# Thirty-eight matmuls instead of 39 per unit of the gate and up products: features split 192, 64, 192

## The chip, the cores and the metric

The kernel runs as one program on one core of one Trainium2 chip. Times are device microseconds (us) of one execution; the kernel before took 699.87 us (median of 3 runs, 699.38 to 700.0). The profile is of one further execution. Engines are named as the profile names them: PE (matrix multiplies), PEld (the loads of its stationary operand), DVE (vector), ACT (scalar, activation), POOL (general), SP (issues the DMAs).

## The reference

One block of a transformer, on x of 2048 tokens by 448 features, all in fp32. First a Fourier mixing layer, real part only, and a residual; then a gated feed-forward layer (GEGLU, 448 to 1792 to 448 features) and a residual:

```python
n = layernorm(x)
a, b = n @ dft_hid_re.T, n @ dft_hid_im.T
h = x + dft_seq_re @ a - dft_seq_im @ b
m = layernorm(h)
g, u = m @ w_gate, m @ w_up
out = h + (gelu_tanh(g) * u) @ w_down
```

Matrix products on PE are made in fp16. An fp32 operand is split into a high and a low half (hi = fp16(a), lo = fp16(a - hi)), and a product of two fp32 operands is three fp16 products: hi·hi, hi·lo, lo·hi. Where a layer's sizes allow, a Strassen-like scheme makes seven block products instead of eight.

## The kernel before, in words

**Stages.** The program has four stretches in order of time. (1) The sequence transform, 64 steps (`N_STEPS`), the last 32 of them with seven products ("fast"); PE multiplies blocks of the sequence matrices (`ws`, halves made from `wr`) by the halves of the normalised x. Between its steps stand, for 7 of the 8 token pairs p, the hidden transform (`hid_mm`, 21 matmuls for each half g of the pair), the second layer norm, and the preparation of the feed-forward operands. (2) Gate and up products for token block 0 (512 tokens), 14 units t = 0 to 13, one for each slice of 128 features. (3) Gate and up for blocks 1 and 2 (256 tokens each), 28 units, with the down products between them. (4) The rest of the down products. A unit is thus 512 columns wide 14 times and 256 columns wide 28 times.

**A unit** (class `GateUp`) makes seven products into three banks X, Y and Z, in the order x1 (A11·B11), z1 (S1·T1), y1 (S2·T2), x2 (A12·B21), z2 (S4·B22), y2 (S3·T3), y3 (A22·T4), y3 after x1 and z1 of the next unit. Between two of them ACT or DVE takes the bank's value: after x1 ACT copies X to Y (L1089), and y1 adds to that copy.

**The 448 features** are the contracted dimension, split 256 and 192. Products over 256 take two slots of 128 rows and 3 terms, so 6 matmuls; products over 192 take one and a half slots and so 5 matmuls, the halves of two terms sharing one slot. Four products of 6 and three of 5 make 39.

**Operands.** Activations: for each token pair ACT writes the normalised pair to `xn` (`ffn_norm_act`), DVE makes differences in `tt` (`ffn_sums`), ACT writes high halves to `xs` (`ffn_hi`, helper `hi_part`, L108), DVE low halves (`ffn_lo`, helper `lo_part`, L112 without a scale, L114 with one), and SP transposes `xs` into `hops` (25 slots). Weights: class `Weights` loads a feature slice (`gu_raw`), makes sums on DVE (`gu_s`, L328 to L331), high halves on ACT and low halves on DVE (`gu_w`, 28 slots), and stores them. Eight slices are prepared in stretch 1, six in stretch 2.

**What sets the order.** Nothing is scheduled by a tool: the order in the code is the order of each engine's queue, and an engine runs its queue strictly in that order. In stretch 1 tables `early` and `after` attach work to a step n: `early[n]` runs after the step's own `ws` halves, `after[n, half]` after each half of the step's matmuls. The tables of slices (`DFT_F`: slice f has its sums at step n, raw halves at n+1, halves of sums at n+2) and of pairs (`ffn_sums` and `ffn_split` at n1 and n2) fill them. For the first pair n1, n2 are 22 and 23, and slice 5 has n = 22. `hid_out(p, g)` (L719 to L721 on ACT) takes the result of `hid_mm(p, g)`, and `hid_seed(p, 1)` (L711 on ACT) then puts h back into the same bank; `hid_mm(p, 1)` can begin only after that.

Of the kernel before, what the change touches and what calls it, by code (L numbers as in the profile page):

```python
# [13 lines left out]
P = 128  # L14
# [18 lines left out]
def kernel(  # L33
# [127 lines left out]
    OPS_K1 = {"B11": 0, "T1": 4, "T2": 8, "T3": 12}  # L161
    OPS_K2 = {"B21": 16, "B22": 19, "T4": 22}
    N_OPS = 25


    W_OPS = {"A11": 0, "A12": 2, "A22": 4, "S1": 6, "S2": 8, "S3": 10, "S4": 12}
# [79 lines left out]
    def ffn_sums(q, j, parts=range(4)):  # L246

        if 0 in parts:
            t = fops.tile([P, 960], F32, tag="tt", name=f"tt_{q}_{j}")
            ffn[q, j] = ffn[q, j], t  # L250
        xn, t = ffn[q, j][:2]
        sub = V.tensor_sub
        if 0 in parts:
            sub(t[:, 0:256], xn[:, 1, 0:256], xn[:, 0, 0:256])
        if 1 in parts:
            sub(t[:, 256:448], xn[:, 1, 256:448], t[:, 0:192])
            V.tensor_scalar(t[:, 448:512], t[:, 192:256], -1.0, None, op0=ALU.mult)
        if 2 in parts:
            sub(t[:, 512:704], xn[:, 1, 256:448], xn[:, 1, 0:192])
            V.tensor_scalar(t[:, 704:768], xn[:, 1, 192:256], -1.0, None, op0=ALU.mult)  # L260
        if 3 in parts:

            sub(t[:, 768:960], xn[:, 0, 256:448], t[:, 256:448])

    def ffn_views(q, j):
        xn, t, xs = ffn[q, j]
        k1 = xs[:, 0:2048].rearrange("p (o h d) -> p o h d", o=4, h=2)
        k2 = xs[:, 2048:3200].rearrange("p (o d) -> p o d", o=3)
        return xn, t, k1, k2, t[:, 0:768].rearrange("p (o d) -> p o d", o=3)

    def ffn_hi(q, j, parts=range(2)):
        if 0 in parts:
            ffn[q, j] += (fops.tile([P, N_OPS * P], F16, tag="xs", name=f"xs_{q}_{j}"),)
        xn, t, k1, k2, t3 = ffn_views(q, j)
        if 0 in parts:
            hi_part(k1[:, 0, 0, :], xn[:, 0, 0:256])
            hi_part(k2[:, 0:2, 0:192], xn[:, :, 256:448])
        if 1 in parts:
            hi_part(k1[:, 1:4, 0, :], t3)
            hi_part(k2[:, 2, 0:192], t[:, 768:960])  # L280

    def ffn_lo(q, j, parts=range(5)):
        xn, t, k1, k2, t3 = ffn_views(q, j)
        raw, t4 = (k2[:, 0:2], xn[:, :, 256:448]), (k2[:, 2], t[:, 768:960])
        if 0 in parts:
            lo_part(k1[:, 0, 1, :], xn[:, 0, 0:256], k1[:, 0, 0, :])
        if 1 in parts:
            lo_part(k1[:, 1:4, 1, :], t3, k1[:, 1:4, 0, :])
        for n, (dst, src) in ((2, raw), (4, t4)):
            if n in parts:  # L290
# [1295 lines left out]
```

## Time and profile before

| | |
|---|---|
| median of 3 runs | 699.87 us |
| span of the profiled execution, first to last instruction | 698.1 us |
| outside that span (median less span) | 1.8 us |
| PE busy | 693.5 us, 5308 matmuls |
| DVE busy | 571.2 us, 1137 instructions |
| ACT busy | 394.1 us, 781 instructions |
| POOL busy | 166.6 us |
| stretch 1, to about | 337 us |
| stretch 2, to about | 462 us |

The profiled execution has no time of its own beside the span; the 1.8 us is the difference to the median of the timed runs. In the timeline of an engine a row is: start in us, length in us, engine, line, operation, out<-in by the names of the program, shapes, and how many instructions were merged into the row; in brackets stands how long the engine was idle ahead of it and what ended that. Rows of one engine can overlap by some tens of nanoseconds, since an instruction begins before the one ahead has quite ended.

### The profile page before, as it was taken

How to read it: one execution, taken by the hardware profiler on the slowest of the kernel's cores; microseconds unless marked ns; L12 is line 12 of the kernel's file. 1: busy time of each engine (PE TensorE's matmuls, PEld its weight loads, DVE VectorE, ACT ScalarE, POOL GpSimd, SP SyncE). 2: the span in 40 equal slices, each digit the busy share in tenths (PEclk: the TensorE clock that was granted, in tenths of full speed). 3: DMA queues.
4: the chain of work that ended last, by engine and by line, in shares of the span. 5: the costliest groups of instructions: out<-in, count | busy, mean ns of one | idle time of the engine just before them, and what ended most of it. 6: DMA issues, size and time to landing. Idle time of an engine off the chain costs nothing.

```text
span 698.1 us, 13955 instructions
## 1 busy us (share of the span) xinstructions
PE 693.5 (99%) x5308; PEld 514.3 (74%) x5308; DVE 571.2 (82%) x1137; ACT 394.1 (56%) x781; POOL 166.6 (24%) x183
## 2 busy tenths in 40 slices
PE   9999999999999999999999999999999999999998
PEld 6555555555979888997644444469999999999997
DVE  6998996958999898995648797777778877899786
ACT  5876755746766555665427666555555453655631
POOL 0004754461202000000303333521120111232224
PEclk9999999999999999999999999999999999999999
DMA  8798679997968559384656877797869985887612
GB/s 272 243 244 271 143 260 268 249 251 286 194 197 189 163 125 237 127 196 178 158 187 239 286 235 247 202 325 237 234 206 334 243 300 176 313 283 273 226 50 80
DMA packets 113731, 155.81 MB, mean 223 GB/s; under 512 B 61696, under 2 KB 78208, under 8 KB 113664
## 3 DMA queue, kind: packets, MB, share of 16 engines
q1 hardware_dynamic: 113664, 154.92, 74.1%
q8 instruction: 41, 0.67, 0.4%
q14 instruction: 26, 0.21, 0.1%
HBM read 106.66 MB, written 34.34 MB: 202 GB/s over the span
## 4 chain that ended last, share of the span: by engine, by line
PE 96%; ACT 1%; DVE 1%; issue 1%; POOL 0%; ACTq 0%; POOLq 0%
PE acc L644 21%; PE acc_f L521 16%; PE acc_d L1248 15%; PE pY L1044 15%; PE pZ L1044 10%; PE pX L1044 10%; PE y L730 9%; PE pw L102 1%; ACT ws L108 1%; DVE ws L114 0%; ACT xn_h L243 0%; DVE sums L471 0%; ACT dn_w L108 0%; ACT v L974 0%; ACT y L721 0%
## 5 line engine op out<-in xcount | busy, mean ns | idle before, releaser
L1044 PEld LDWEIGHTS <-gw 128*128 128x128 f16 x1365 | 133.3, 98 | 42.7
L644 PE MATMUL acc<-xs,ws 128*128 128x448 f16 x768 | 146.9, 353 | 0.0
L521 PEld LDWEIGHTS <-ws 128*128 128x128 f16 x1344 | 128.7, 98 | 2.2 <-DVE ws L114 0.5
L644 PEld LDWEIGHTS <-ws 128*128 128x128 f16 x768 | 75.3, 98 | 70.3 <-issue 0.6
L1138 POOL TENSOR_TENSOR hs<-hs,c 128x256 f32<-128x256 f32 (+1 forms) x42 | 59.2, 1410 | 248.2 <-ACT c L1136 181.7
L1248 PE MATMUL acc_d<-wd,dn_w 128*128 128x224 f16 x1008 | 110.7, 259 | 0.0
L1248 PEld LDWEIGHTS <-dn_w 128*128 128x128 f16 x1008 | 96.9, 98 | 2.0
L521 PE MATMUL acc_f<-t,ws 128*128 128x224 f16 x768 | 92.2, 259 | 0.1
L1044 PE MATMUL pY<-hops,gw 128*128 128x256 f16 (+1 forms) x595 | 90.2, 294 | 0.0
L114 DVE SCALAR_TENSOR_TENSOR ws<-wr,ws 128x768 f16<-128x768 f32 (+2 forms) x66 | 73.8, 1119 | 10.4 <-ACT ws L108 10.1
L521 PE MATMUL acc_f<-xs,ws 128*128 128x224 f16 x576 | 73.5, 259 | 0.0
L108 ACT ACTIVATE ws<-wr 128x768 f16<-128x768 f32 (+2 forms) x66 | 60.4, 916 | 11.9 <-DMA wr<-in_w_seq_dram 11.0
L730 PE MATMUL y<-wh,z 128*128 128x448 f16 x336 | 66.2, 352 | 0.0
L1044 PE MATMUL pZ<-hops,gw 128*128 128x256 f16 (+1 forms) x385 | 61.7, 294 | 0.0
L1044 PE MATMUL pX<-hops,gw 128*128 128x256 f16 (+1 forms) x385 | 61.7, 294 | 0.0
L1089 ACT ACTIVATE pY<-pX 128x256 f32<-128x256 f32 (+1 forms) x42 | 18.4, 439 | 66.9 <-PE pX L1044 66.5
L730 PEld LDWEIGHTS <-z 128*128 128x128 f16 x336 | 32.9, 98 | 29.5 <-issue 0.3
L108 ACT ACTIVATE ws<-sums 128x512 f16<-128x512 f32 x64 | 39.0, 624 | 25.4 <-DVE sums L471 18.1
L1044 PEld LDWEIGHTS <-gu_w 128*128 128x128 f16 x273 | 26.6, 98 | 31.9
L1054 DVE SCALAR_TENSOR_TENSOR c<-pZ,u 128x256 f32<-128x256 f32 (+1 forms) x42 | 21.5, 511 | 34.7 <-PE pZ L1044 17.9
L1100 ACT ACTIVATE u<-pY 128x256 f32<-128x256 f32 (+1 forms) x42 | 19.1, 454 | 53.6 <-PE pY L1044 53.5
L112 DVE TENSOR_TENSOR dn_w<-dn_s,dn_w 128x640 f16<-128x640 f32 x48 | 42.2, 879 | 1.5 <-ACT dn_w L108 1.4
(148 smaller groups left out, 1005.1 us busy)
## 6 DMA issues: line engine op xcount, KB each, us to landing
gw<-w_dram SPq DMA_DIRECT2D x35, 896.0 KB, 6.6
wr<-in_w_seq_dram SPq DMA_DIRECT2D x100, 256.0 KB, 4.2
hid_dram<-hs SPq DMA_DIRECT2D x27, 512.0 KB, 5.9
hid<-hid_dram SPq DMA_DIRECT2D x54, 256.0 KB, 5.6
w_dram<-gu_w SPq DMA_DIRECT2D x14, 896.0 KB, 5.2
gu_raw<-in_w_gu_dram SPq DMA_DIRECT2D x28, 384.0 KB, 5.4
wr<-in_w_seq_dram SPq DMA_DIRECT2D x14, 512.0 KB, 5.7
x<-in_x_dram SPq DMA_DIRECT2D x16, 224.0 KB, 4.3
```

Source lines behind the costliest of these rows:

```text
L108: A.activation(dst, src, AF.Copy, scale=scale)
L112: V.tensor_sub(dst, src, hi)
L114: V.scalar_tensor_tensor(dst, src, scale, hi, op0=ALU.mult, op1=ALU.subtract)
L521: PE.matmul(fast_sum(n, k), fast_a(n, i, lw, a), fast_b(j, lx, b), start=j == 0 and m == 0 and k in (0, 1, 3, 5), stop=j == NT // 2 - 1 an ...
L644: PE.matmul(acc[key][:, :D], w[:, lw, block * P : (block + 1) * P], xs[c][:, lx, :], start=c == 0 and m == 0, stop=c == NT - 1 and m == 2,)
L730: PE.matmul(y[:, :D], z[p][:, lz, k, g * P : (g + 1) * P], wh[:, lw, k, :], start=p == NP - 1 and k == 0 and m == 0, stop=k == 6 and m == ...
L1044: PE.matmul(ps, w[:, wl, wa + ws, :], ops[:, m + ms, :], start=first and n == 0, stop=last and n == len(terms) - 1, skip_group_check=True,)
L1054: V.scalar_tensor_tensor(dst, ps, SC, other, op0=ALU.mult, op1=ALU.add)
L1089: A.activation(self.Y, self.X, AF.Copy)
L1100: A.activation(self.u2, self.Y, AF.Copy, scale=SC)
L1138: G.tensor_mul(c22, c22, self.cols(self.c12))
L1248: PE.matmul(ps, w[:, la, a, :], wd[n][:, lb, b, :], start=n == 0 and m == 0 and opens, stop=n == NC - 1 and m == 2, skip_group_check=True,)
```

## The change

The 448 features are split 192, 64 and 192. Every product contracts over 192, and the middle 64 rows are a further product that isn't made by itself: its three half-size terms ride in the empty halves of the slots of S1, S2 and S3's operands and of the A and S4 products. S1, S2, S3 and A11 take 5 matmuls, A12, A22 and S4 take 6 (`W_TERMS`): 38 in all. `hops` and `xs` have 27 slots.

To fill the slots the preparation changes:

- `Weights.tails` (ACT, two casts of 64 partitions) at step n-1 of a slice; one more such cast at the head of `hi(True)`; `rest` (DVE, one operation of 64 partitions) after the raw low halves. The difference L330 is 384 wide instead of 256. The halves of sums take two casts of 768 and 640 instead of two of 512 on ACT, and four operations (384, 384 on 64 partitions, 128 on 64 partitions, 256) instead of two of 512 on DVE.
- `ffn_sums` makes four differences of 192 and, as part 3, one of 64 that reads a high half already made. `ffn_split` no longer makes all high halves and then all low ones: high part 0, low part 0, high part 1, sums part 3, low parts 1 and 2, high part 2, low part 3.
- `ffn_transpose` moves 8, 3, 4 and 12 slots instead of 8, 8, 6 and 3; the plan of side work in stretches 2 and 3 is put in the new order of parts, at the same places.

The places in the order on which the prediction rests come from here. **ACT, step 23**, the high halves of the first pair (xs from xn and tt) up to the seed of the second half of pair 1 (L711, y_1). Before:

```order
L108 ACTIVATE xs_0_1459<-tt_0_1404 128x3x256
L108 ACTIVATE xs_0_1459<-tt_0_1404 128x192
L108 ACTIVATE zs_1201<-acc_10_1251 128x448
L108 ACTIVATE zs_1201<-acc_11_1252 128x448
L108 ACTIVATE ws_1509<-wr_1389 128x1024
L108 ACTIVATE gu_w_1454<-gu_s_1399 128x512 x2
L719 ACTIVATE hx_1_1268,mv_h_1_1564<-y_0_1411 128x448
L720 ACTIVATE mv_h_1_1564<-mv_h_1_1564 128x1
L721 ACTIVATE y_0_1411,mv_h_1_1564<-y_0_1411,mv_h_1_1564 128x448
L711 ACTIVATE y_1_1568<-hx_1_1268 128x448
```

Now, from the first cast of the new high part 2 (gu_raw_1395 is the next slice's raw tile):

```order
L108 ACTIVATE xs_0_1485<-tt_0_1430 128x256
L108 ACTIVATE xs_0_1485<-xs_0_1485 128x64
L108 ACTIVATE zs_1217<-acc_10_1269 128x448
L108 ACTIVATE gu_raw_1395<-gu_raw_1395 64x128 x2
L108 ACTIVATE zs_1217<-acc_11_1270 128x448
L108 ACTIVATE ws_1542<-wr_1413 128x1024
L108 ACTIVATE gu_w_1478<-gu_s_1425 128x768
L108 ACTIVATE gu_w_1478<-gu_s_1425 128x640
L754 ACTIVATE hx_1_1288,mv_h_1_1599<-y_0_1435 128x448
L755 ACTIVATE mv_h_1_1599<-mv_h_1_1599 128x1
L756 ACTIVATE y_0_1435,mv_h_1_1599<-y_0_1435,mv_h_1_1599 128x448
L746 ACTIVATE y_1_1603<-hx_1_1288 128x448
```

The first of these rows reads the last 64 columns of tt, which DVE now writes inside the split, and the second reads a low half that DVE writes; behind them stand the same zs, ws, gu_w and L719 to L721 work as before (now L754 to L756 and L746), with two casts of a raw tile between.

**DVE, the same step.** Before, from the ws low half (its differences tt stood ahead of this row):

```order
L114 SCALAR_TENSOR_TENSOR ws_1451<-wr_1334,ws_1451 128x1024
L114 SCALAR_TENSOR_TENSOR gu_w_1454<-gu_raw_1205,gu_w_1454 128x512
L114 SCALAR_TENSOR_TENSOR gu_w_1454<-gu_raw_1205,gu_w_1454 128x256
L112 TENSOR_TENSOR xs_0_1459<-xn_h_0_1355,xs_0_1459 128x256
L112 TENSOR_TENSOR xs_0_1459<-tt_0_1404,xs_0_1459 128x3x256
L112 TENSOR_TENSOR xs_0_1459<-xn_h_0_1355,xs_0_1459 128x2x64
L112 TENSOR_TENSOR xs_0_1459<-xn_h_0_1355,xs_0_1459 128x2x128
```

Now:

```order
L114 SCALAR_TENSOR_TENSOR ws_1475<-wr_1354,ws_1475 128x1024
L114 SCALAR_TENSOR_TENSOR gu_w_1478<-gu_raw_1223,gu_w_1478 128x512
L114 SCALAR_TENSOR_TENSOR gu_w_1478<-gu_raw_1223,gu_w_1478 128x256
L377 SCALAR_TENSOR_TENSOR gu_s_1425<-gu_w_1478,gu_raw_1223 64x128
L112 TENSOR_TENSOR xs_0_1485<-xn_h_0_1377,xs_0_1485 128x2x64
L112 TENSOR_TENSOR xs_0_1485<-xn_h_0_1377,xs_0_1485 128x2x192
L272 TENSOR_TENSOR tt_0_1430<-xn_h_0_1377,xs_0_1485 128x64
L112 TENSOR_TENSOR xs_0_1485<-tt_0_1430,xs_0_1485 128x3x192
```

The row L272 (sums part 3) is what ACT's cast of 256 above waits for; six DVE rows of this step now stand ahead of it.

**ACT, step 17**, slice 9's raw high halves up to the seed of the second half of pair 0. Before:

```order
L108 ACTIVATE gu_w_1184<-gu_raw_1002 128x512
L108 ACTIVATE gu_w_1184<-gu_raw_1002 128x256
L108 ACTIVATE zs_1201<-acc_00_1027 128x448
L719 ACTIVATE hx_0_980,mv_h_0_1229<-y_0_1096 128x448
L720 ACTIVATE mv_h_0_1229<-mv_h_0_1229 128x1
L721 ACTIVATE y_0_1096,mv_h_0_1229<-y_0_1096,mv_h_0_1229 128x448
L711 ACTIVATE y_1_1233<-hx_0_980 128x448
```

Now:

```order
L108 ACTIVATE gu_raw_1008<-gu_raw_1008 64x128
L108 ACTIVATE gu_w_1198<-gu_raw_1008 128x512
L108 ACTIVATE gu_w_1198<-gu_raw_1008 128x256
L108 ACTIVATE zs_1217<-acc_00_1033 128x448
L108 ACTIVATE gu_raw_1123<-gu_raw_1123 64x128 x2
L754 ACTIVATE hx_0_984,mv_h_0_1247<-y_0_1106 128x448
```

The new first row overwrites a part of the raw tile that the first of slice 9's sums on DVE (now L354) reads, so ACT waits there for DVE, which it did not before.

The diff, cut to its core:

```diff
+    W_TERMS = {
+        "A11": ((0, 0), (17, 0), (1, 1), (18, 1), (0, 2)),
+        "A12": ((3, 0), (20, 0), (2, 1), (19, 1), (3, 2), (2, 3)),
...
+        "S1": ((7, 0), (23, 0), (8, 1), (7, 2), (6, 3)),
...
     def ffn_sums(q, j, parts=range(4)):
...
-            sub(t[:, 0:256], xn[:, 1, 0:256], xn[:, 0, 0:256])
+            sub(t[:, 0:192], xn[:, 1, H1], xn[:, 0, H1])
         if 1 in parts:
-            sub(t[:, 256:448], xn[:, 1, 256:448], t[:, 0:192])
-            V.tensor_scalar(t[:, 448:512], t[:, 192:256], -1.0, None, op0=ALU.mult)
+            sub(t[:, 192:384], xn[:, 1, H1], xn[:, 1, H2])
+            sub(t[:, 384:576], xn[:, 1, H2], t[:, 0:192])
         if 2 in parts:
-            sub(t[:, 512:704], xn[:, 1, 256:448], xn[:, 1, 0:192])
-            V.tensor_scalar(t[:, 704:768], xn[:, 1, 192:256], -1.0, None, op0=ALU.mult)
+            sub(t[:, 576:768], xn[:, 0, H2], t[:, 384:576])
         if 3 in parts:
-            sub(t[:, 768:960], xn[:, 0, 256:448], t[:, 256:448])
+            xs = ffn[q, j][2]
+            sub(t[:, 768:832], xn[:, 0, RR], xs[:, 7 * P + 192 : 7 * P + 256])
...
+        if 2 in parts:
+            hi_part(t4[:, 0], t[:, 576:832])
+            hi_part(ts[:, 0, 1, 192:256], b2[:, 1, 1, 192:256])
...
     def ffn_split(q, j):
-        ffn_hi(q, j)
-        ffn_lo(q, j)
+        ffn_hi(q, j, (0,))
+        ffn_lo(q, j, (0,))
+        ffn_hi(q, j, (1,))
+        ffn_sums(q, j, (3,))
+        ffn_lo(q, j, (1, 2))
+        ffn_hi(q, j, (2,))
+        ffn_lo(q, j, (3,))
...
+        def tails(self):
+            gate, up = self.raw
+            hi_part(gate[64:, 3], gate[64:, 0])
+            hi_part(gate[64:, 0], up[64:, 3])
...
-            V.tensor_sub(s[:, 6:8], gate[:, 0:2], up[:, 0:2])
-            V.tensor_sub(s[:, 8:10], gate[:, 4:6], s[:, 4:6])
+            V.tensor_sub(s[:, 6:9], up[:, 0:3], gate[:, 0:3])
+            V.tensor_sub(s[:, 9:11], gate[:, 3:5], s[:, 3:5])
...
         def hi(self, of_raw):
             if of_raw:
                 self.w = w_tile(f"gu_w{self.f}", self.place)
+                hi_part(self.up[64:, 3], self.up[64:, 0])
...
+        def rest(self):
+            a2 = self.slots(4, 5)[64:, 0]
+            V.scalar_tensor_tensor(self.s[64:, 9], a2, -1.0 / W_SC, self.gate[64:, 3], op0=ALU.mult, op1=ALU.add)
...
+            w, s = self.slots(0, 28), self.s
+            lo_part(w[:, 23:26], s[:, 1:9:3], w[:, 7:15:3], W_SC)
+            for k in slice(8, 15, 3), slice(12, 13):
+                lo_part(w[64:, k], s[64:, k.start - 6 : k.stop - 6 : k.step], w[64:, k], W_SC)
+            lo_part(w[:, 26:28], s[:, 9:11], w[:, 15:17], W_SC)
...
         def split(self, of_raw):
             self.hi(of_raw)
             self.lo(of_raw)
+            if of_raw:
+                self.rest()
...
+        at(after, (n - 1, 0), lambda f=f: gu[f].tails())
...
-            at(early, n1, lambda b=b, j=j: ffn_sums(b, j))
+            at(early, n1, lambda b=b, j=j: ffn_sums(b, j, range(3)))
...
-        for n, (wl, ws, ms) in enumerate(terms):
+        for n, (wo, m) in enumerate(W_TERMS[a]):
             PE.matmul(
                 ps,
-                w[:, wl, wa + ws, :],
-                ops[:, m + ms, :],
+                w[:, wo, :],
+                ops[:, OPS[b] + m, :],
```

More of the change, by code (lines that the diff above doesn't have):

```diff
@@ L275, in ffn_hi @@
         if 0 in parts:
[L276 to L277 removed]
+            hi_part(b2[:, :, 0, 192:256], xn[:, :, RR])
+            hi_part(b2[:, :, 0, 0:192], xn[:, :, H2])
+            hi_part(xs[:, 0:192], xn[:, 0, H1])
         if 1 in parts:
[L279 to L284, printed above, removed]
+            hi_part(ts[:, :, 0, 0:192], t3)
@@ L1352 @@
         if w:
+            w.rest()
             w.hi(False)
```

108 lines of the change are left out of this document (54 added, 54 removed), and 4 rows, old and new, of the table W_TERMS.

## The prediction

> **What bounds the kernel now.** I read the page's first part, then PE's waits, then the chain of work that ended last, then stretches, then the timeline of each engine at the few places where PE comes close to waiting.
>
> ```profile
> PE 693.5 (99%) x5308; PEld 514.3 (74%) x5308; DVE 571.2 (82%) x1137; ACT 394.1 (56%) x781; POOL 166.6 (24%) x183
> ...
> PE pw L102 <- POOL sign_t L93: 1.4, 1, 1.4
> PE acc_d L1248 <- ACT v L974: 0.2, 1, 0.2
> ```
>
> PE is busy from end to end: its waits (line <- releaser: us in total, times, longest) are 1.4 us at the start and 0.2 us near the end. So any matmul that goes saves its full spacing, as long as no other engine starts to be late. That "as long as" is the whole question, because the change adds work to DVE and ACT. Stretch 2 (from : to, length, then PE, PEld, DVE, ACT and POOL busy, PEclk, DMA share, GB/s):
>
> ```profile
> 337.00:462.00 125.00, 125.00 (x589) 57.40 (x588) 93.06 (x152) 71.69 (x126) 39.04 (x32) 1.00 0.74 232
> ```
>
> There DVE has 32 us free and ACT 53; what is added there (casts and differences of six slices, a few tenths of a us each) is paid from that. In stretch 1 an order of much tighter waits decides, below.
>
> **What is saved.** Matmuls follow each other at a fixed spacing; I take it from the starts of rows:
>
> ```profile
> 336.80 1.46 PE L1044 MATMUL pX<-hops,gu_w 128*128 128x512 f16 x6
> 338.09 1.46 PE L1044 MATMUL pZ<-hops,gu_w 128*128 128x512 f16 x6
> 339.39 1.46 PE L1044 MATMUL pY<-hops,gu_w 128*128 128x512 f16 x6
> ...
> 477.91 1.36 PE L1044 MATMUL pY<-hops,gw 128*128 128x256 f16 x11
> 479.11 0.82 PE L1044 MATMUL pZ<-hops,gw 128*128 128x256 f16 x6
> ```
>
> Six matmuls of 512 columns take 339.39 - 338.09 = 1.30, or 0.216 each; eleven of 256 take 1.20, or 0.109 each. One fewer in each of 14 + 28 units: 14 x 0.216 + 28 x 0.109 = 3.02 + 3.05 = **6.1 us saved**. The removed weight loads lie beside PE's matmuls (PEld 57 of 125 us there) and count nothing. The two other slots of `hops` cost transposes on SP, with no wait of PE on them in the profile: zero, or, if they came late, part of the wait of the first unit below.
>
> **What is given back.** In stretch 1 the new casts and differences stand in the queues of ACT and DVE ahead of work PE waits for. PE's rows there, with the two that give the hidden transform's second halves (103.57 and 134.22):
>
> ```profile
> 69.70 25.53 PE L644 MATMUL acc<-xs,ws 128*128 128x448 f16 x134
> 95.06 4.14 PE L730 MATMUL y<-wh,z 128*128 128x448 f16 x21
> ...
> 103.57 4.13 PE L730 MATMUL y<-wh,z 128*128 128x448 f16 x21
> ...
> 134.22 2.06 PE L730 MATMUL y<-wh,z 128*128 128x448 f16 x10
> ```
>
> *First place, 79.2 us.* The spacing here is (95.06 - 69.70) / 134 = 0.1893; the first matmul of token pair 2 stands 84 matmuls before 95.06, at 79.17, and it needs the bank that is free when DVE has made the first zs low half from it.
>
> ```profile
> 74.20 0.88 DVE L330 TENSOR_TENSOR gu_s<-gu_raw 128x256 f32<-128x256 f32 x1
> ...
> 78.51 1.67 DVE L114 SCALAR_TENSOR_TENSOR zs<-acc,zs 128x448 f16<-128x448 f32 x3
> ```
>
> Three such halves take 1.67, so the first is done about 79.1: nothing to spare. DVE runs without a gap from L330, and L330 grows from 256 to 384 elements: 0.88 x 0.5 = 0.44, and the new 64-partition difference adds about 0.2. Give **0.6** (0.3 at the price of the 0.41 row below, 1.0 if each costs as much as a 0.88 row's half more).
>
> *Second place, 103.57.* The second half of pair 0 waits for ACT's seed L711.
>
> ```profile
> 93.79 0.94 ACT L108 ACTIVATE gu_w<-gu_raw 128x512 f16<-128x512 f32 x2 [1.08 <-DMA w_dram<-gu_w]
> ...
> 99.29 0.55 ACT L719 ACTIVATE hx<-y 128x448 f32<-128x448 f32 x1 [3.49 <-PE y L730]
> ...
> 100.95 0.55 ACT L711 ACTIVATE y<-hx 128x448 f32<-128x448 f32 x1
> ...
> 98.01 0.90 DVE L328 TENSOR_TENSOR gu_s<-gu_raw 128x384 f32<-128x384 f32 x1
> ```
>
> The seed ends at 101.50, 2.07 early. Now the raw halves of slice 9 (93.79) stand behind a cast that waits for DVE's L328, which ended at 98.91. DVE itself is later by the additions of slices 13 and 11: 0.44, 0.2 and about 0.4 for 1152 instead of 1024 elements of low halves of sums, then about 0.9 again, 1.9 in all. Then 100.8, one cast (0.2), the raw halves 0.9, zs 0.5, two casts (0.4): L719 at 102.8 instead of 99.29, and the seed, 2.21 later, at 105.0. PE, late by 0.6, wants it at 104.2: **0.8** (0 if DVE's slack before L328 takes its lateness, 1.5 if POOL slows it more).
>
> *Third place, 134.22, the large one.* The seed L711 for the second half of pair 1 ended at 133.83, 0.39 early. The whole chain ahead of it:
>
> ```profile
> 117.98 1.25 DVE L114 SCALAR_TENSOR_TENSOR ws<-wr,ws 128x1024 f16<-128x1024 f32 x1 [3.34 <-ACT ws L108]
> 119.15 2.21 DVE L114 SCALAR_TENSOR_TENSOR gu_w<-gu_s,gu_w 128x512 f16<-128x512 f32 x2
> ...
> 122.86 0.41 DVE L330 TENSOR_TENSOR gu_s<-gu_raw 128x256 f32<-128x256 f32 x1
> ...
> 124.37 1.25 DVE L254 TENSOR_TENSOR tt<-xn_h 128x256 f32<-128x256 f32 x1
> ...
> 127.95 1.68 DVE L114 SCALAR_TENSOR_TENSOR ws<-wr,ws 128x1024 f16<-128x1024 f32 x1
> 129.55 1.19 DVE L114 SCALAR_TENSOR_TENSOR gu_w<-gu_raw,gu_w 128x512 f16<-128x512 f32 x2
> 130.66 0.41 DVE L112 TENSOR_TENSOR xs<-xn_h,xs 128x256 f16<-128x256 f32 x1
> 131.00 0.95 DVE L112 TENSOR_TENSOR xs<-tt,xs 128x768 f16<-128x768 f32 x1
> ...
> 122.90 2.44 POOL L575 TENSOR_TENSOR tx<-xs 128x448 f32<-128x448 f16 x2
> ```
>
> ```profile
> 127.79 1.10 ACT L108 ACTIVATE xs<-tt 128x768 f16<-128x768 f32 x2 [1.76 <-DVE tt L260]
> 128.79 0.96 ACT L108 ACTIVATE zs<-acc 128x448 f16<-128x448 f32 x2
> 129.64 1.06 ACT L108 ACTIVATE ws<-wr 128x1024 f16<-128x1024 f32 x1
> 130.59 1.15 ACT L108 ACTIVATE gu_w<-gu_s 128x512 f16<-128x512 f32 x2
> 131.63 0.54 ACT L719 ACTIVATE hx<-y 128x448 f32<-128x448 f32 x1
> ...
> 133.28 0.55 ACT L711 ACTIVATE y<-hx 128x448 f32<-128x448 f32 x1
> ...
> L108 ACT ACTIVATE xs<-tt 128x768 f16<-128x768 f32 x8 | 6.7, 834 | 1.8 <-DVE tt L260 1.8
> L108 ACT ACTIVATE dn_w<-dn_s 128x640 f16<-128x640 f32 x48 | 34.9, 727 | 12.1 <-DVE dn_s L1210 12.0
> L108 ACT ACTIVATE xs<-tt 128x192 f16<-128x192 f32 x8 | 2.8, 351 | 0.0
> ```
>
> Before, ACT's casts of the pair waited only for the differences tt, made in one run at 124.37 to 127.95. Now the cast of 256 waits for the last difference (L272 of the change), and that stands behind six DVE operations. DVE: it starts the 117.98 operation 0.4 late (two casts of 128 elements ahead of ACT's ws half, 0.2 each between starts: the 192-element cast has 0.35, and neighbours overlap by 0.1); 1152 instead of 1024 elements at 119.15: +0.4; L330 of 384: +0.2; differences of 768 instead of 960 elements: 3.58 x 0.8 = 2.87, -0.7. So the ws half begins at 128.2 instead of 127.95. It and the raw halves take until 130.9 (130.66 + 0.3), the 64-partition difference 0.2, then 512 elements of low halves about 0.7 (0.95 for 768), L272 0.2: **132.0**. ACT: the cast of 256 and one of 64 take 0.5, so zs begins at 132.5 instead of 128.79. Then zs 0.85, two casts 0.4, ws 0.95, halves of sums 0.83 + 0.73 less 0.1 of overlap, 1.45: L719 at 136.15, and the seed 2.2 later, 138.35. PE wants it at 134.22: **4.1 us**. This chain is tied to PE's earlier progress (L719 after pair 0 opens the layer norm whose result pair 0's casts use), so it moves with the first two waits and adds to them. Bounds: 1.5, worked out in the first rival, and 5.0, if L330, the differences and the low halves each meet POOL once more at 0.3 on average.
>
> Behind this one row of the trace stands a price I can't fix: 256 elements cost DVE 0.41 at 122.86 and 1.25 at 124.37, while POOL's row of 2.44 runs. The Trainium skill, "SBUF — State Buffer", section "Who interferes with whom", says that a DVE instruction with two SBUF inputs contends with a GpSimd one that reads SBUF, and that the second to issue waits for the whole of the first; the trace's 1.25 against 0.41 agrees. By it the price goes by meetings, not by elements: one meeting more or fewer is 0.84, so 3.3 to 4.9 for the 4.1.
>
> *Small ones.* ACT's copy of X to Y in a unit stood between x1's end and y1's start with z1's six matmuls to hide it; now x1 and z1 have five each, so y1 is wanted 0.43 earlier.
>
> ```profile
> 338.49 0.58 ACT L1089 ACTIVATE pY<-pX 128x512 f32<-128x512 f32 x1
> 421.86 0.57 ACT L1089 ACTIVATE pY<-pX 128x512 f32<-128x512 f32 x1
> ```
>
> The first unit's copy ended at 339.07 for 339.39: 0.32 - 0.43 = -0.1, plus overlap, **0.15**. The copy at 421.86 stands in a stretch where ACT's additions weigh 0.8 for a slice: **0.2**. The wait at L1248 near the end grows by the same 0.1: **0.1**. Elsewhere (the other tight places of stretch 1 come after 134 us) PE arrives later than before by the stalls, which makes them looser. Nothing to several tenths more: 0 to 1.
>
> **Sum.** -6.1 + 0.6 + 0.8 + 4.1 + 0.45 = -0.15. The span of the profiled execution is 698.1; the median 699.87 lies 1.8 above it and I take that outside part as unchanged: **699.7 us**, as good as no change.
>
> **Rivals.** *The gain comes through.* DVE runs at its cheap prices (0.41 for 256 elements, 1.25 for the ws half of 1024, 1.19 for 768 of low halves): then the differences take 1.1 instead of 2.87, and 1152 elements of low halves 1.8 instead of 2.6, which makes the third wait 4.1 - 2.6 = 1.5; with half the first two (0.7) and 0.45 that is -3.4, so **696.5**; with no wait left at all 693.8. For it: most of DVE's rows elsewhere show these prices. Against it: POOL works on tx through this very stretch, before as after, and the cast's wait on L272 is in the order whatever DVE's price. Three in ten.
>
> *Slower.* PE's clock. The program's first matmuls, of 128 columns, run at half pace:
>
> ```profile
> 0.00:6.00 6.00, 4.65 (x44) 4.65 (x45) 2.30 (x9) 2.59 (x5) 0.85 (x9) 1.00 0.59 171
> ```
>
> 4.65 / 44 is 0.106 each, where the spacing of 448 columns (0.1893) gives 0.054. If a pause of some 4 us at 134 puts PE back into that, the next 5 us of matmuls take twice their time: 2.5 to 2.9 more, so **702.4**. It decides if the pause is longer than some length that this trace can't show, since its only pauses are 1.4 and 0.2. The PEclk column reads 1.00 in that slow stretch too, so the spacings have to be read. Two in ten, with longer waits than I priced. The Trainium skill, "TensorE: Matmul & The Clock Gate", Part 1 on the HAM clock gate, states that the array falls to half rate after one idle window of about 3.4 us that runs freely. By that rule a pause of 4.1 catches a whole window about one time in five (an estimate from the page's figure), and at 5 about half the time; no pause here is long enough to show it.
>
> That the change doesn't do what it says I exclude: the order has 38 matmuls in each unit.
>
> **How the numbers follow.** Forecast 0.5, own range 698.3 to 701.2; the first rival 0.3; the second 0.2. A measurement here tells 0.2% or 1.4 us from no change: faster is the first rival and the forecast's lower tail, 0.33; slower the second rival and a little of the forecast's upper edge, 0.23; the rest, 0.44, same. The range 696.4 to 702.5 takes in the centres of both rivals.
>
> **What would show it.** PE's waits in the changed profile should name ACT's seed (y <- ACT y L746) at about 104 and 134 us, together some 5 us, the second the larger; PE's units should be 38 matmuls at the same spacing. ACT's row ahead of it should wait for DVE's tt L272 at 132. Right rows but another length is my price of DVE; no wait at 134 would make the forecast wrong and the first rival right; matmuls of 448 columns spaced 0.37 behind the pause are the second.

## The result, and the profile after

The changed kernel takes **707.46 us** (median of 4 runs, 707.13 to 709.11) beside 699.62 for the kernel before in the same comparison. The ratio is put at 1.0119, 95% interval 1.0105 to 1.0134; like all ratios below it is an estimate from the single runs, not the quotient of the two medians. The changed kernel is 7.8 us slower, where 699.7 and no change were forecast. The page of the changed kernel and its table of PE's waits (line <- releaser: us in total, times, longest):

```profile
span 705.9 us, 13987 instructions
...
PE 689.8 (98%) x5266; PEld 510.4 (72%) x5266; DVE 587.9 (83%) x1171; ACT 418.4 (59%) x855; POOL 164.9 (23%) x183
```

```profile
PE y L765 <- ACT y L746: 7.6, 2, 5.6
PE pY L1072 <- ACT u L1128: 1.5, 2, 1.0
PE pw L102 <- POOL sign_t L93: 1.4, 1, 1.4
PE pY L1072 <- DVE hs L1082: 1.1, 2, 0.7
PE acc L679 <- DVE zs L114: 0.9, 1, 0.9
PE pY L1072 <- ACT pY L1117: 0.4, 1, 0.4
```

PE has 42 matmuls fewer and is 3.7 us less busy, yet the span grew by 7.8: about 11 us are waits that the kernel before didn't have. ACT's seed makes 7.6 of them, at the two places that the prediction named; another 3 us stand in stretch 2 (line 1072), where hardly any were expected. PE's timeline of the changed kernel, at the places that the prediction quoted of before:

```profile
95.53 4.14 PE L765 MATMUL y<-wh,z 128*128 128x448 f16 x21
...
106.23 1.11 PE L765 MATMUL y<-wh,z 128*128 128x448 f16 x5 [2.03 <-ACT y L746]
...
142.64 5.70 PE L765 MATMUL y<-wh,z 128*128 128x448 f16 x21 [5.61 <-ACT y L746]
148.18 2.05 PE L679 MATMUL acc<-xs,ws 128*128 128x448 f16 x10
...
346.24 1.24 PE L1072 MATMUL pX<-hops,gu_w 128*128 128x512 f16 x5
```

Against the rows of before the starts have moved by 95.53 - 95.06 = 0.5, 106.23 - 103.57 = 2.7, 142.64 - 134.22 = 8.4 and 346.24 - 336.80 = 9.4. The row at 142.64 also shows something else. Its 21 matmuls take 5.54 to the next row where 21 x 0.189 = 3.97 is their pace. For 3 us PE ran at half pace behind the long wait. The sums, as forecast and as the starts of the two traces give them, in us:

| term | forecast | measured |
|---|---|---|
| 42 matmuls removed | -6.1 | -6.0 |
| first place, 79 us | +0.6 | +0.5 |
| second place, 106 us | +0.8 | +2.2 |
| third place, 142.6 us | +4.1 | +5.8 |
| half pace behind it | 0 (the slower rival: 2.5 to 2.9) | +1.6 |
| units of stretch 2 and the rest of the small ones | +0.45 | +4.0 |
| small waits of before that went, and others | 0 | -0.3 |
| sum | -0.15 | +7.8 |

A wait costs PE some 0.17 more from start to start than the idle time that the table of waits gives. In stretch 2, for instance:

```profile
429.17 1.24 PE L1072 MATMUL pZ<-hops,gw 128*128 128x512 f16 x5
431.12 1.46 PE L1072 MATMUL pY<-hops,gu_w 128*128 128x512 f16 x6 [0.71 <-DVE hs L1082]
```

From 429.17 to 431.12 is 1.95 where five matmuls take 1.08: 0.87 for a wait of 0.71. The 3.0 of stretch 2 in six waits (with the first unit's copy) are 4.0 so. The wait at 79 is 1.0 from start to start, but half of it only gives back what PE had won at the program's start, where the slow first matmuls ended 0.5 earlier in this execution than in that of before; in other executions with a later end of that phase there is no wait at 79 at all.

### The profile page after: what moved, and what is told of

Same layout as the page of the kernel before. It is cut to its first block, busy times and chain, and to the rows that moved or that the text cites. A ratio compares the mean times of both kernels' runs of the same rounds, so it can differ in the third digit from the quotient of the medians.

```text
span 705.9 us, 13987 instructions
## 1 busy us (share of the span) xinstructions
PE 689.8 (98%) x5266; PEld 510.4 (72%) x5266; DVE 587.9 (83%) x1171; ACT 418.4 (59%) x855; POOL 164.9 (23%) x183
## 5 line engine op out<-in xcount | busy, mean ns | idle before, releaser
L1072 PEld LDWEIGHTS <-gw 128*128 128x128 f16 x1330 | 129.8, 98 | 44.6 <-issue 3.4
L1072 PE MATMUL pY<-hops,gw 128*128 128x256 f16 (+1 forms) x560 | 85.6, 294 | 2.3 <-ACT u L1128 1.5
L765 PE MATMUL y<-wh,z 128*128 128x448 f16 x336 | 67.7, 358 | 7.6 <-ACT y L746 7.6
L1128 ACT ACTIVATE u<-pY 128x256 f32<-128x256 f32 (+1 forms) x42 | 19.0, 453 | 40.4 <-PE pY L1072 40.1
```

Source lines behind the costliest of these rows:

```text
L765: PE.matmul(y[:, :D], z[p][:, lz, k, g * P : (g + 1) * P], wh[:, lw, k, :], start=p == NP - 1 and k == 0 and m == 0, stop=k == 6 and m == ...
L1072: PE.matmul(ps, w[:, wo, :], ops[:, OPS[b] + m, :], start=first and n == 0, stop=last and n == len(W_TERMS[a]) - 1, skip_group_check=True,)
L1128: A.activation(self.u2, self.Y, AF.Copy, scale=SC)
```

## The experiments

The times that follow are medians, each set beside runs of the kernel before on the same chip (698.9 to 699.3 there); the changed kernel's own ratio for comparison is 1.0119.

**The split of the first pair, its last part two steps later.**

```diff
-            at(early, n2, lambda b=b, j=j: ffn_split(b, j))
+            late = 2 if p == 0 else 0
+            at(early, n2, lambda b=b, j=j: ffn_split(b, j, 0))         # hi 0, lo 0, hi 1
+            at(early, n2 + late, lambda b=b, j=j: ffn_split(b, j, 1))  # sums 3, lo 1 and 2, hi 2, lo 3
             for k in range(4):
-                at(after, (n2 + 1 + k // 2, k % 2), ...ffn_transpose...)
+                at(after, (n2 + 1 + k // 2 + late // 2, k % 2), ...ffn_transpose...)
```

> The changed kernel with one thing moved: for the first token pair the last part of the split (sums part 3, low parts 1 and 2, high part 2, low part 3) stands at step 25 instead of 23, with its transposes one step later. Theory 'order' (ACT's cast of 256 waits for DVE's L272 and holds everything behind it): zs, at 136.30 in the changed kernel's ACT timeline, follows the casts that end at 133.26, so the wait for the seed at 142.6 falls from 5.6 to about 2.6 us and PE keeps its full pace behind it: 707.5 - 3.0 - 1.6 = 702.9. Theory 'price' (DVE itself is late there by its costs, whatever the order): the wait stays above 4.5 us, half pace stays, 706 to 707.5.

Measured: 706.17, ratio 1.0112 (1.0091 to 1.0134). PE's row at the third place and two of its waits in this run:

```profile
139.74 4.13 PE L767 MATMUL y<-wh,z 128*128 128x448 f16 x21 [2.50 <-ACT y L748]
...
PE y L767 <- ACT y L748: 4.9, 3, 2.5
PE acc_f L558 <- DVE ws L114: 0.9, 2, 0.5
```

The wait fell from 5.6 to 2.5, as the order theory said to a tenth, and in this execution the 21 matmuls keep their pace. So 3.1 of the 5.6 is the moved part, with ACT's cast behind L272. But the time hardly moved, and the 702.9 of that theory was missed: of the 4.7 won there, waits that the changed kernel does not have took back 2.2 in the sequence transform, from start to start (on ws, and a third one on a seed, at 175), and the place at 79 another 0.2. PE now arrives earlier at places whose margin had only been the delay. This run's span, 703.7, is 2.2 below the changed kernel's; its other runs were up to 3.5 us longer than the profiled one, so its median doesn't show even that. Their granted clock is 0.998, 0.997 and 0.995 where the profiled one has 1.000; the changed kernel's trace, with 3.4 us at half the clock, has 0.997, and the traces of the next two experiments, with 6.8 us, have 0.995. So the other three very likely had the half pace, and the profiled one escaped it by luck (see the pauses below).

**ACT's new casts out of the way of the seeds.**

```diff
-        at(after, (n - 1, 0), lambda f=f: gu[f].tails())
+        at(after, (n - 1, 1), lambda f=f: gu[f].tails())
...
-        at(early, n + 1, lambda f=f: gu[f].split(True))
+        if f != 9:
+            at(early, n + 1, lambda f=f: gu[f].split(True))
+    at(after, (19, 0), lambda: gu[9].split(True))     # behind hid_out(0, 0) and hid_seed(0, 1)
```

> The changed kernel with ACT's new casts taken out of the way of the seeds: the split of slice 9's raw halves stands behind the seed of pair 0's second half (step 19) instead of ahead of it, and the two tail casts of each slice stand half a step later. Theory 'order': the wait at 106 (2.0 us) goes, and that at 142.6 falls by the two tails' 0.6: 707.5 - 2.2 - 0.6 = 704.7. Rival: DVE gets slice 9's work later and is late by as much at the next place: the wait at 142.6 grows by what the one at 106 loses, 707.

Measured: 704.78, ratio 1.0084 (1.0069 to 1.0099). The wait at 106 is gone; the one at 140 stays at 5.6, neither shorter by the tails (half a step later they still stand ahead of that seed) nor longer. So slice 9's cast behind DVE's L354 was the whole second wait, and the third is not fed by it. The 704.7 expected was met in part by luck: the 0.6 for the tails didn't come, but this trace has no wait at 79, which hangs on the program's start.

**The price by instruction.** The changed kernel makes the low halves of a slice's sums with four DVE operations instead of two. Two of them again, on the changed kernel, and four instead of two on the kernel before. (With two, two of the slots get the low halves of other sums, so that kernel doesn't compute the block; it serves to read the time.)

```diff
# changed kernel
-            lo_part(w[:, 23:26], s[:, 1:9:3], w[:, 7:15:3], W_SC)
-            for k in slice(8, 15, 3), slice(12, 13):
-                lo_part(w[64:, k], s[64:, k.start - 6 : k.stop - 6 : k.step], w[64:, k], W_SC)
-            lo_part(w[:, 26:28], s[:, 9:11], w[:, 15:17], W_SC)
+            lo_part(w[64:, 8:15:2], s[64:, 2:9:2], w[64:, 8:15:2], W_SC)
+            lo_part(w[:, 23:28], s[:, 6:11], w[:, 12:17], W_SC)
# kernel before
-                lo_part(self.slots(1, s0, s1, src), src, self.slots(0, s0, s1, src), W_SC)
+                for k in slice(0, n), slice(n, 2 * n):      # n: half of the part's columns
+                    lo_part(dst[:, k], src[:, k], hi[:, k], W_SC)
```

> The changed kernel with the low halves of a slice's sums made by two DVE operations (640 elements, and 512 on 64 partitions) instead of four (384, 384 and 128 on 64 partitions, 256): the same number of elements. The values are not those of the reference, since two of the slots get the low halves of other sums. Theory 'price by instruction': the DVE group falls from 41.5 us (56 instructions) to about 28; the waits at 106 and 142.6 shrink by 1 to 1.5 each and those of stretch 2 by about 2: near 703. Theory 'price by element': the group stays above 38 us and the time within 1 us of 707.5. Theory 'order': the group may fall, but the waits at 142.6 stays above 5, near 706.

> The kernel before with one thing done: the low halves of a slice's sums in four DVE operations of 256 elements instead of two of 512. Theory 'price by instruction': the DVE group goes from 26.1 us to about 36, and since the waits at 79 and 134 had margins of 0.05 and 0.39, the time goes up by 1 to 3 us, to 701 to 703. Theory 'price by element': the group is 27 to 29 us (28 more fixed costs of some 0.06) and the time within 0.5 us of before.

Measured: 703.91, ratio 1.0071 (1.0056 to 1.0086), and 700.21, ratio 1.0018 (1.0009 to 1.0028). The groups of these operations (out<-in, shape, count | busy us, mean ns) in the kernel before, the changed one, the changed one with two operations, and the kernel before with four:

```profile
L114 DVE SCALAR_TENSOR_TENSOR gu_w<-gu_s,gu_w 128x512 f16<-128x512 f32 x28 | 26.1, 974 | 2.5 <-ACT gu_w L108 2.5
```

```profile
L114 DVE SCALAR_TENSOR_TENSOR gu_w<-gu_s,gu_w 64x384 f16<-64x384 f32 x14 | 13.7, 975 | 0.3
...
L114 DVE SCALAR_TENSOR_TENSOR gu_w<-gu_s,gu_w 128x256 f16<-128x256 f32 x14 | 10.1, 720 | 0.4
...
L114 DVE SCALAR_TENSOR_TENSOR gu_w<-gu_s,gu_w 128x384 f16<-128x384 f32 x14 | 8.9, 637 | 0.6
L114 DVE SCALAR_TENSOR_TENSOR gu_w<-gu_s,gu_w 64x128 f16<-64x128 f32 x14 | 8.8, 630 | 0.0
```

```profile
L114 DVE SCALAR_TENSOR_TENSOR gu_w<-gu_s,gu_w 128x640 f16<-128x640 f32 x14 | 17.2, 1229 | 0.5
L114 DVE SCALAR_TENSOR_TENSOR gu_w<-gu_s,gu_w 64x512 f16<-64x512 f32 x14 | 11.6, 826 | 0.8
```

```profile
L114 DVE SCALAR_TENSOR_TENSOR gu_w<-gu_s,gu_w 128x256 f16<-128x256 f32 x56 | 31.4, 620 | 2.0 <-ACT gu_w L108 2.0
```

41.5 us in the changed kernel against 26.1 before, for an eighth more elements per partition (1152 for 1024, and 512 of them on only 64 partitions); 28.8 with two operations. Price by instruction holds on the changed kernel, and 3.5 us of its time hang on it: the second wait halves (from 2.0 to 0.9) and of the 4.0 of stretch 2 only 1.4 is left, from start to start. The third stays at 5.3, so it is a matter of order, not of this price. On the kernel before, four operations cost 5.3 us of DVE and 1.2 us of time, less than price by instruction said (36) and more than price by element: 16 of the 56 took 0.58 to 1.49, the other 40 the 0.41 to 0.43 of one alone.

Where the price comes from is seen in one group beside POOL's row. DVE and POOL of the changed kernel, twice the same four operations:

```profile
430.98 1.80 DVE L114 SCALAR_TENSOR_TENSOR gu_w<-gu_s,gu_w 128x384 f16<-128x384 f32 x4
...
447.33 4.51 DVE L114 SCALAR_TENSOR_TENSOR gu_w<-gu_s,gu_w 128x384 f16<-128x384 f32 x4
...
447.65 1.36 POOL L1166 TENSOR_TENSOR hs<-hs,c 128x512 f32<-128x512 f32 x1 [6.40 <-ACT c L1164]
448.97 1.44 POOL L232 TENSOR_TENSOR wd_s<-wd 128x448 f32<-128x448 f32 x1
450.38 1.18 POOL L234 TENSOR_TENSOR wd_s<-wd 128x448 f32<-128x448 f32 x1
451.52 0.83 POOL L235 TENSOR_TENSOR wd_s<-wd 128x224 f32<-128x224 f32 x1
```

With POOL idle the four take 1.80; beside four POOL operations they take 4.51. The first of them (0.55) is still without POOL, the other three take 1.51, 1.22 and 1.24, about one POOL operation each. So an operation of 64 x 128 elements, 0.28 when alone, costs over 1.2 in such company, nearly as much as one three times its size.

**Both moves together, and the order of stretch 2.** First the two edits above in one kernel; then, on top of it, pair q = 2's last parts one unit later and the last pair's residual ahead of the low halves of sums; then that with two operations:

```diff
-    AT_A += ((2, 1), (2, 3), (2, 3), (3, 1), (2, 4), (3, 1), (2, 4), (3, 4))
+    AT_A += ((2, 1), (2, 3), (2, 3), (3, 1), (3, 1), (3, 2), (3, 1), (3, 4))
...
         cur.x1()
+        if t == 2:
+            hid_add(NP - 1, 1)
+            ffn_moments(NB - 1, 1, hp[NB - 1, 1], 1)
         if w:
             w.lo(False)
```

> The edits of the two runs e1_split and e4_seed together on the changed kernel, nothing else. If the waits are independent: those at 79 and 106 go (-3.2), that at 142.6 falls to 2.5 or less and the half pace goes (-4.7): 707.4 - 7.9 = 699.5, as before. If time won there is taken back where DVE and ACT come late for the fast steps (e1_split showed new waits at 175, 199, 259 and 260, 1.3 us in all, once PE came 4.7 us earlier): these grow by up to the 2.6 by which PE comes earlier still, 700.8 to 703.5. The waits of stretch 2 (4 us) stay.

> c0_both with the order of stretch 2 changed too: the last parts of a pair's split (high part 2, low part 3) one unit later, behind the unit's own casts, and the residual and moments of the last pair on DVE ahead of the low halves of a slice's sums. Theory 'order': the waits at 385, 389 and 454 of the changed kernel go (2.4 us), those at 431 and 433 (1.4) stay: 2.4 below c0_both. Theory 'price': DVE is late there by the four operations at up to 4.5 us whatever the order; the waits move to other units and less than 1 us is won.

> c1_jit with the low halves of sums in two DVE operations as in e2_lo2 (two slots get other sums' low halves, so the values are not the reference's): what is left of DVE's price by instruction on top of the order. If most of what c1_jit has above the matmuls' own 694 is that price, it comes to 695 to 697 (below before); if not, it stays within 1 us of c1_jit.

Measured: 702.91 (ratio 1.0058, 1.0043 to 1.0073), 702.09 (1.0046, 1.0029 to 1.0063) and 697.91 (0.9982, 0.9973 to 0.9992). Together the two moves win 4.6, more than the 1.3 and the 2.7 that each wins alone, but far less than the 7.9 of all the waits that they were meant to remove: in the trace the wait at 79 and the half pace are still there, and the latent waits came up (258 to 260 and 292 show them). The order of stretch 2 removed the waits of the units at 385, 389 and 454, but one of 1.0 at 467 came up instead, so the medians differ by 0.8 and not by 2.4. That 0.8 lies within the scatter of the runs (701.0 to 704.8 with the new order); in the traces stretch 2 gives back 2.5 instead of 4.0. With two operations another 4.2 us go, part of it the half pace (1.7 us in the trace before, none in this one). That is below the kernel before, though above the 695 to 697 expected, and for a kernel that doesn't compute the block.

**Pauses on the kernel before**, to see when PE falls to half pace:

```diff
         y = ys[p, g] = ps_tr.tile(...)
+        for _ in range({1: 12, 2: 17, 3: 22, 4: 27, 5: 32}.get(p, 0) if g else 0):
+            A.activation(warm, eps_t, AF.Copy)
```

> The kernel before with 12, 17, 22, 27 and 32 idle ACT operations of about 0.2 us ahead of the seed of the second half of pairs 1 to 5, so that PE pauses for some 2, 3, 4, 5 and 6 us (less where ACT had slack). Theory 'clock' (a long pause drops PE to half pace): after the longest pauses matmuls of 448 columns are spaced 0.37 instead of 0.19 for some 3 us, after 2 us (as at 106 in the changed kernel) not, and the point from which it happens is seen. Rival (the half pace at 142.6 came from something else, such as operands arriving late): all matmuls behind the pauses keep 0.19.

Measured: 718.23, in a single run. PE's timeline has pauses of 2.0, 1.2, 4.6 and 3.6 us (in the two long ones PE waits for ACT's ws halves, which stand in ACT's queue behind the idle operations); the first and the last of them, and for comparison the third place in the run with stretch 2's order:

```profile
135.94 4.13 PE L732 MATMUL y<-wh,z 128*128 128x448 f16 x21 [2.03 <-ACT y L713]
...
303.80 0.55 PE L521 MATMUL acc_f<-xs,ws 128*128 128x224 f16 x2 [3.60 <-ACT ws L108]
304.80 2.05 PE L521 MATMUL acc_f<-xs,ws 128*128 128x224 f16 x10 [0.44 <-DVE ws L114]
306.64 3.47 PE L521 MATMUL acc_f<-t,ws 128*128 128x224 f16 x18
```

```profile
136.58 5.82 PE L767 MATMUL y<-wh,z 128*128 128x448 f16 x21 [2.26 <-ACT y L748]
```

After 2.03 the pace is full; after 3.60 ten matmuls of 224 columns take 1.84 (306.64 - 304.80), 0.184 each, where 0.096 is their pace; after 2.26 about half of the 21 are slow (5.82 instead of 4.13), and so they are after 2.67 in the run of both moves. But after 2.50, in the run with the split moved, the pace was full. The granted clock (PEclk; columns as in the prediction's row of stretch 2) shows both the half pace and why a shorter pause can do what a longer one doesn't. First the run with stretch 2's order, then the one with the split moved:

```profile
133.22:136.63 3.41, 1.15 (x7) 0.53 (x6) 3.40 (x7) 3.31 (x9) 0.00 (x0) 1.00 0.99 296
136.63:140.04 3.41, 3.41 (x10) 1.37 (x10) 3.31 (x8) 3.05 (x6) 0.00 (x0) 0.50 0.94 337
```

```profile
135.60:139.01 3.41, 1.64 (x9) 0.75 (x8) 3.41 (x6) 3.35 (x8) 0.00 (x0) 1.00 0.84 276
139.01:142.42 3.41, 2.69 (x15) 1.40 (x15) 3.29 (x9) 3.33 (x7) 0.00 (x0) 1.00 0.94 290
```

In these traces the clock goes to 0.50 and back only a whole number of times 3.41 us after its first record, where the slow start ends (6.92 us in the first, 5.89 in the second); the rows above are such windows. At the end of a window in which PE had idled 2.26 us or more the clock dropped in every trace, and never after one with 1.99 or less. The pause of 2.26 lay whole in one window; the one of 2.50 was cut into 1.77 and 0.73. Half pace then lasted one window or, where PE idled 1.19 or more in the next window too, two. So the clock theory holds, but the length of the pause decides only together with where the windows fall, and that differs between executions.

**Orders that keep 38 matmuls.** Three versions, each meant to remove the waits that the one before left. The first has the whole split of pair 0 at step 25, the second its sums at 24 and pair 3 at 57 and 58, the third slice 0's halves of sums at step 35; all of them keep the moves of the casts (slice 9, the tails) and of stretch 2 and make the first down operand's halves (`dn_hi(0)`, `dn_lo(0)`) ahead of the last unit's c and hs. The second also has the norm of a late pair half a unit later in stretch 2; the third puts it back:

```diff
-            n0, n1, n2 = ((21, 22, 23), (27, 28, 32), (36, 37, 38), (44, 45, 46))[p]
+            n0, n1, n2 = ((21, 22, 25), (27, 28, 32), (36, 37, 38), (44, 46, 47))[p]   # first
+            n0, n1, n2 = ((21, 24, 25), (27, 28, 32), (36, 37, 38), (44, 57, 58))[p]   # second, third
...
-            at(early, n + 3, lambda: gu[0].split(False), ...)
+            at(early, n + 5, lambda: gu[0].split(False), ...)                          # third
```

> The changed kernel's 38 matmuls with the order of the side work changed as the runs so far point to: as c1_jit, but the whole split of the first pair at step 25 (not only its last part), pair 3's sums and split one step later (46 and 47), and the first down operands' halves ahead of the last unit's own c and hs on DVE. If the third wait is made of DVE's differences and ACT's casts of them (c1_jit: ACT waits 2.77 us for the differences at 129.3), it goes whole, and the half pace with it: 2.4 + 1.7 off; the waits at 256 (0.9) and 467 (1.2) go too: c1_jit's 702.1 - 6.2 = 696, below before by 0.4%. Rival (what is won is taken back by DVE at the price of four operations per slice): new waits of 2 us or more appear in the fast steps and in stretch 2, 698 to 700, not to be told from before.

> d1_order with three more moves: the first pair's sums one step before its split (24, 25), since in d1_order ACT's second cast of halves of sums waits 3.06 us for the 64-partition difference that stands behind them; the fourth pair's sums and split at steps 57 and 58, where PE waited for nothing; the norm of a late pair half a unit later, behind the copy that y1 needs. If the waits left in d1_order are such single collisions, they go: 1.2 at 135, 1.4 at 262 to 268, about 1 at 423 and 425, and the median falls from 698.9 to 695.5 to 696.5, 0.4 to 0.5% below before. If DVE is simply short of time there, waits of the same size appear next to the old ones and the time stays at 698.5 to 699.5.

> d2_order with the norm of a late pair back where d1_order had it, and the halves of slice 0's sums two steps later (35, a step without halves of sequence operands on DVE at its head). In d2_order stretch 1 waits only at 192.6 (1.2 us over the matmuls' spacing, DVE's ws low halves behind the four operations of slice 0); stretch 2 waits 4.6 us, 1.6 of it at 432.8 behind the moved norm, where d1_order waited 2.2. If these are single collisions: 192.6 goes, stretch 2 is as in d1_order, 699.5 - 1.2 - 2.4 = 696, 0.4% below before. If DVE is short of time, waits of about the same sum turn up in other units, as in d2_order: 698.5 to 699.5.

Measured: 698.85 (ratio 1.0001, 0.9989 to 1.0012), 699.50 (1.0005, 0.9996 to 1.0014) and **698.08 (0.9982, 0.9973 to 0.9991)**. In the first, the third wait fell to 1.0; what ACT waited for there had become the new 64-partition difference on DVE:

```profile
132.54 0.74 ACT L108 ACTIVATE gu_w<-gu_s 128x640 f16<-128x640 f32 x1 [3.06 <-DVE gu_s L377]
```

In the second that wait was gone whole, but the norm moved in stretch 2 made a new one of 1.4 at 432.8, and the time didn't fall. In the third, PE's largest waits are

```profile
PE pw L102 <- POOL sign_t L93: 1.3, 1, 1.3
PE acc_f L556 <- DVE ws L114: 0.7, 2, 0.4
PE pY L1074 <- DVE hs L1084: 0.6, 2, 0.3
```

and no half pace is left after the start. It is below the kernel before by 0.18%, some 1.3 us of the 6.1 that the matmuls are worth. That is less than the 696 or so expected of each of the three if the waits left were single collisions: the first two came out where the rival had them (new waits elsewhere, since DVE is short of time), the third between the two. What is missing stands in the third's trace as small waits, 2.7 us from start to start in stretch 1 (from 70 us on) and 1.7 in stretch 2, where the kernel before gives back 0.5 and nothing. The same moves on the kernel before, as far as it has a place for them:

> The kernel before, 39 matmuls per unit, with those moves of d3_order that it has a place for: slice 9's raw halves behind the seed, the first pair's sums and split at 24 and 25, the fourth pair's at 57 and 58, slice 0's halves two steps later, the last residual ahead of the low halves of sums, the first down halves earlier. If what d3_order wins over before comes from the 42 removed matmuls, this kernel is as before, within 0.2%, since PE waited there for 1.6 us in all. If the moves themselves win, it is faster by as much as d3_order, 0.18%, or 1.3 us.

Measured: 698.80 beside 698.85, ratio 0.9998 (0.9989 to 1.0007). As far as the interval tells, the moves by themselves win nothing: what the third order wins comes from the removed matmuls.

## Why the prediction was wrong, point by point

**What was right.** The saving (6.0 of 6.1), the three places, the engine that PE would wait for at each, and the direction of the chain: ACT's cast behind L272 was 3.1 of the third wait. First place: 0.5 for 0.6, in part by luck, since there is a wait at all only where PE's slow start ends early.

**Second place: 2.2 for 0.8.** The step that failed is DVE's lateness there. DVE's and ACT's rows of the changed kernel:

```profile
97.24 3.48 DVE L114 SCALAR_TENSOR_TENSOR gu_w<-gu_s,gu_w 128x384 f16<-128x384 f32 x4
100.76 0.61 DVE L354 TENSOR_TENSOR gu_s<-gu_raw 128x384 f32<-128x384 f32 x1
...
101.46 0.31 ACT L108 ACTIVATE gu_raw<-gu_raw 64x128 f32<-64x128 f32 x1 [4.66 <-DVE gu_s L354]
...
103.18 0.64 ACT L108 ACTIVATE gu_raw<-gu_raw 64x128 f32<-64x128 f32 x2
```

I gave slice 11's low halves of sums 2.2 + 0.4, by elements; four operations beside POOL took 3.48. L354 ended at 101.4 instead of the forecast 100.8, and ACT's three casts of 64 x 128 took 0.95 instead of 0.6.

**Third place: 5.8 for 4.1**, above the upper bound of 5.0. The chain as forecast, each of its starts moved by the 2.7 that PE was late: the sequence operand's half on DVE at 130.9, the difference L272 done at 134.7, zs at 135.2, L754 (the former L719) at 138.8. Measured:

```profile
121.89 1.23 DVE L114 SCALAR_TENSOR_TENSOR ws<-wr,ws 128x1024 f16<-128x1024 f32 x1 [4.16 <-ACT ws L108]
...
125.86 1.27 DVE L354 TENSOR_TENSOR gu_s<-gu_raw 128x384 f32<-128x384 f32 x1
...
130.09 0.81 DVE L263 TENSOR_TENSOR tt<-xn_h 128x192 f32<-128x192 f32 x1
...
132.41 1.22 DVE L114 SCALAR_TENSOR_TENSOR ws<-wr,ws 128x1024 f16<-128x1024 f32 x1
...
135.57 0.22 DVE L272 TENSOR_TENSOR tt<-xn_h,xs 128x64 f32<-128x64 f32 x1
...
135.83 0.42 ACT L108 ACTIVATE xs<-tt 128x256 f16<-128x256 f32 x1 [2.56 <-DVE tt L272]
...
140.41 0.52 ACT L754 ACTIVATE hx<-y 128x448 f32<-128x448 f32 x1
```

The first sum in the kernel before, for comparison (the differences followed at 124.37):

```profile
121.40 0.90 DVE L328 TENSOR_TENSOR gu_s<-gu_raw 128x384 f32<-128x384 f32 x1
```

DVE began the half at 132.4, 1.5 later than forecast. The earlier half at 121.89 was already 0.8 later than forecast (117.98 + 0.4 + 2.7 = 121.1), since it waited for ACT: ACT's two casts ahead took 0.7 instead of 0.4, and the new operation L377 on DVE (0.3) stands ahead of the layer norm's chain that ACT waits for, a place where I had put it at nothing. The four sums L354 to L357 then took 4.2 (125.86 to 130.09) where before they took 3.0 and I had forecast 3.2; another part of POOL's work lay beside them. I had taken the prices of before with the alignment of before, 0.41 for L330 among them. The differences gave 0.6 of this back (2.3 for 2.9). The rest of the way to L272's end was faster than forecast, 3.4 for 3.8, and ACT's casts behind it 0.5 slower.

**Half pace: 1.6 for none.** This was the slower rival, with its mechanism and its place right and its price (2.5 to 2.9) too high; I gave it two in ten. It needs the long wait first, so it was part of the forecast's own tail rather than a case beside it. By the rows of the pauses it belonged in the sum. A pause of 4.1 leaves 2.26 or more of idle time in one window of 3.41 unless an edge falls between 1.84 and 2.26 us behind the pause's start; that is 0.42 of 3.41, so the half pace was to be expected nearly nine times in ten (an estimate from those rows). The prediction's one time in five asked for a window idle from end to end.

**Stretch 2: 4.0 for 0.45**, the largest miss. The step that failed is "what is added there is paid from" DVE's 32 and ACT's 53 free us, an average over 125 us. Two rows of ACT in the changed kernel, and the first of them in the kernel before:

```profile
384.56 0.30 ACT L129 ACTIVATE sd_h_last<-mv_h,eps_t 128x2 f32<-128x2 f32 x1 [2.62 <-DVE mv_h L205]
...
453.14 0.42 ACT L108 ACTIVATE xs<-tt 128x256 f16<-128x256 f32 x1 [4.27 <-DVE tt L272]
```

```profile
373.65 0.29 ACT L129 ACTIVATE sd_h_last<-mv_h,eps_t 128x2 f32<-128x2 f32 x1
```

Both are small operations at the head of ACT's queue that wait for DVE, which is inside a group of four low halves at 4.5 us; the unit's own copy u (L1128) stands right behind, and PE's product behind that. ACT idles 2.6 and 4.3 us there and is late all the same. The second wait was added by the change; the first operation was there before and waited for nothing, since DVE's group of two took 2.35 there. I had followed the queues place by place in stretch 1 and not done so for stretch 2. The runs separate the two causes in part: with two operations for four 1.4 of the 4.0 is left, with the order changed 2.5, and with both 0.5. The copy in the first unit, which I did price at 0.15, came out at 0.17 from start to start.

**The price by meetings.** Beside the 4.1 I had set the rule of the Trainium skill, "SBUF — State Buffer", section "Who interferes with whom", and then counted one meeting more or fewer. The rows agree with the page (4.51 beside four POOL operations, 1.80 alone); the count was wrong. Two more operations in each of 14 groups are up to 28 more meetings, and the group cost 15.4 us more of DVE, not an eighth of 26.

## What to carry to other kernels

Count instructions, not elements, for DVE's work beside a busy POOL: four operations for the work of two cost 41.5 us instead of 28.8 in the changed kernel, 31.4 instead of 26.1 in the kernel before. When a strictly ordered queue gets an operation that waits for another engine, price everything behind it, stretch by stretch; the free time of the stretch on average says nothing about it. And a delay upstream hides waits downstream: winning 4.7 us at one place here uncovered 2.2 us of others, so the gain of a fix is read after all of them are out, and removed work on the bound engine is worth its time only as far as its feeders keep up: here 1.3 of 6.1 us, after eight moves.

## What the runs showed that I had not expected

PE's half pace is set off by shorter pauses than I thought, and not by their length alone: 2.26 us idle or more in one of the 3.41 us windows of the granted clock did it every time, 1.99 or less never, so that a pause of 2.26 did it and one of 2.50, cut by a window's edge, didn't. It lasted 3.41 us of granted time after pauses of 2.26, 2.67 and 5.61, and 6.83 after 3.60, 4.61, 5.33 and 5.60. The Trainium skill, "TensorE: Matmul & The Clock Gate", Part 1, gives one idle window of about 3.4 us that runs freely; the length and the free running agree with these traces, but the window need not be idle from end to end, as two thirds of it were enough. The slow phase at the program's start also ended at different times in different executions of nearly the same first steps, 29 to 48 slow matmuls, worth 0.7 us, with a wait at 79 us that appears only when it ends early.
